# Causal scores of nine blocks in column tiles of 32 keys instead of full 128 x 128 products

## The chip, the cores and the metric

The kernel runs on one core of a Trainium2 chip. The metric is device time in microseconds, the median of several executions. One execution was also recorded by the hardware profiler; its spans and waits are read below.

## The reference

A decayed linear attention feeds two feed-forward layers; the second is a mixture of eight experts of which each token takes one.

```python
# attention, batch 4, heads 8, 768 steps, head size 48
mag = np.sqrt(a_re*a_re + a_im*a_im)
scale = np.minimum(mag, 0.999) / (mag + 1e-06)
ar, ai = a_re*scale, a_im*scale
for t in range(S):
    S_re, S_im = ar*S_re - ai*S_im + kv_t, ar*S_im + ai*S_re   # kv_t = outer(k_t, v_t)
    y[:, :, t] = einsum('bhd,bhde->bhe', q_t, S_re)
x = y as (3072, 384)
# first layer
x = ((x @ w_a) * (x @ w_b)) @ w_out          # inner width 1536
# second layer: 8 experts, inner width 1024, the best one per token
out[token] = gate[token] * (relu(x @ w1[e]) @ w2[e])
```

## The kernel before

Tokens go in 12 blocks of 256 (two chunks of 128), three blocks for each of the four batches. For a block, `pre` works out decays and phases on ScalarE, VectorE and GpSimd, so that the recurrence becomes ordinary products of k and q with 96 rows (real and imaginary part), and SP turns k and q by DMA into `kT` and `qT`, head by head. `attn` then makes, for each chunk:

- `sc`: scores of keys against queries, in two groups (`hg`) of four heads, into one PSUM bank of 128 keys x 4 heads x 128 queries. Keys lie on the partitions. The whole 128 x 128 square is computed.
- `mask`: VectorE multiplies the bank by `causal` (-1 for a query not before the key, else 0), one 128 x 128 triangle repeated for four heads, and writes `sm` in SBUF.
- `kn` and `kept`: TensorE turns k back to keys on partitions, ScalarE copies it out. Not needed for the last chunk of a batch.
- `y`: `sm` times v, plus the state times q, into `y_p`, in four column tiles of 32. v lies in `vpad`, head by head padded to 64 columns.
- `xH`, `xL`: the result is split in two parts, for a product of three fp32r terms.
- `kv`, `sum_`, `fade`: the state of the chunk's end, in three column tiles of 32.

The first layer (`up`, `gate_a`, `gate_b`, `gate_H`, `gate_L`, `down`, 12 slices of the inner width) of block j - 1 runs beside the attention of block j. `sc`, `kn`, `kv`, the counts of the routing and, early, the products that fold the gate's weights into `w_out` (`turned`, `folded`) share one ring of three PSUM banks, `p_sc`. 

The order of the instructions on each engine is worked out when the program is built, by the planner `Plan`. Each operation has an engine, a price, the resources that it reads and writes, and a due time `at`. The planner simulates the engines; among the operations that could start first, it takes the one due first. `TIMES` shifts and stretches the due times of each kind of operation (block 4 stands for all blocks from 4 on). `take` and `give` model the banks of a ring. On the chip the engines keep that order and wait by semaphores. After the planned part, the first layer of the last block, the routing of its tokens and the experts follow, merged by hand.

Of the kernel before, what the change touches and what calls it, by code (L numbers as in the profile page):

```python
# [16 lines left out]
HP = 64  # L17
DM, DFF = 384, 1536
# [49 lines left out]
    'high': (-0, 0.89),  # L68
# [10 lines left out]
    ('pre', 4, 0, 0): (39.6, 1),  # L79
    ('pre', 4, 0, 1): (-35.1, 1),  # L80
    ('pre', 4, 0, 3): (-31.5, 1),
# [379 lines left out]
def fast(tc, q, k, v, a_re, a_im, w_a, w_b, w_out, w_gate, w1, w2, out, dram, x2d):  # L461
# [5 lines left out]
    with ExitStack() as mctx, ExitStack() as ctx:  # L467
# [9 lines left out]
        p_sc = sctx.enter_context(tc.tile_pool(name="p_sc", bufs=3, space=bass.MemoryType.PSUM))  # L477
# [3 lines left out]
        causal = const.tile([128, 128], F32, name="causal")  # L481
        nc.gpsimd.memset(causal, -1.0)
        nc.gpsimd.affine_select(out=causal, in_=causal, pattern=[[1, 128]], compare_op=ALU.is_ge, fill=0.0, base=0, channel_multiplier=-1)
# [42 lines left out]
        def counted():  # L526
            sorting["t"] = p_sc.tile([128, NE], F32, tag="sc", name="so_p")
            nc.tensor.matmul(out=sorting["t"], lhsT=ones16, rhs=acc, start=True, stop=True)
# [72 lines left out]
        def route(j, late):  # L601
# [23 lines left out]
            def count():  # L625
# [10 lines left out]
                t = p_sc.tile([128, 2, NE], F32, tag="sc", name="rk_p")  # L636
# [197 lines left out]
        P = Plan({"sc": 3})  # L834
# [28 lines left out]
        def conv(i, f, src, nm, at):  # L863
# [34 lines left out]
            def turned():  # L898

                K["t"] = p_sc.tile([128, 3, C], F32, tag="sc", name="wt_p")  # L900
                for kk in range(3):
                    nc.tensor.transpose(K["t"][:, kk], A32[nm, f][:, kk * C:(kk + 1) * C], ident)
# [5 lines left out]
            def folded():  # L908
                K["t"] = p_sc.tile([128, NE], F32, tag="sc", name="wg_p")
# [8 lines left out]
            P.add("ACT", on("ACT", 384, True), kept, kind="fold", r=[("wt_p", f)], w=["rx"], at=at + 2, give=t)  # L918
            t = P.add("PE", 0.41, folded, kind="fold", r=["rx"], w=[("wg_p", f)], at=at + 3, take="sc")
            P.add("ACT", 0.17, beside, kind="fold", r=[("wg_p", f)], w=[("A32", nm, f)], at=at + 3, give=t)  # L920
# [39 lines left out]
        def up32(f, cs):  # L960
            n = len(cs) * C
            t = G["ab", 0, f] = p_ab.tile([128, 2, BT], F32, tag="ab", name="ab_p")[:, :, 0:n]
# [4 lines left out]
        def down32(f, cs):  # L967
            for i, c in enumerate(cs):
                if f == 0:
                    G["o", 0, c] = p_o.tile([128, DM + NE], F32, tag=f"o{c}", name=f"o{c}")  # L970
                nc.tensor.matmul(out=G["o", 0, c], lhsT=G["g", 0, f][:, i * C:(i + 1) * C], rhs=A32["o", f], start=f == 0, stop=f == NF - 1)  # L971

        def gate_a32(f, cs):
            n = len(cs) * C
            G["g", 0, f] = mo.tile([128, BT], F32, tag="gL", name="g", bufs=3)[:, 0:n]
            nc.scalar.copy(out=G["g", 0, f], in_=G["ab", 0, f][:, 0])
# [74 lines left out]
        def first_moe(lo, hi):  # L1051
# [10 lines left out]
            for m, (f, cs, at, d) in enumerate(todo):  # L1062
# [3 lines left out]
                P.add("DVE", on("DVE", n), lambda f=f: gate_b(0, f), kind=("gate", 0, cs), r=[a], w=[("gL", m)], at=at, alone=False)  # L1066
# [33 lines left out]
        tpad = [ab.tile([96, H, HP], F32, name=f"T{i}") for i in range(2)]  # L1100
        for t in vpad + tpad:
            nc.gpsimd.memset(t[:, :, D:HP], 0.0)

        SRC = dict(re=a_re, im=a_im, q=q, k=k)

        def load_v(j, c, at):
# [3 lines left out]
            P.add("SP", 0.5, go, kind=("v", min(j, 4)), w=[("v", (2 * j + c) % 3)], at=at, size=196)  # L1110

# [204 lines left out]

        def attn(j, t0, t1):
# [6 lines left out]

            for c in range(2):
# [3 lines left out]
                qk = [(x + "T", c, c2, jj) for x in "qk" for c2 in range(2) for jj in range(3)]  # L1329
                v_, T_, To_ = ("v", (2 * j + c) % 3), ("T", (2 * j + c + 1) % 2), ("T", (2 * j + c) % 2)  # L1330
# [253 lines left out]
```

## Time and profile before

| what | value |
|---|---|
| median of 3 runs | 914.72 us (914.06 to 919.48) |
| profiled execution, its own time | 914.04 us |
| its span, first to last instruction | 912.2 us |
| mean granted TensorE clock | 0.992 |
| TensorE busy | 850.9 us, 93% |
| VectorE, ScalarE, GpSimd busy | 557.2, 477.2, 352.5 us |

Busy time counts how long an engine had something in work; with an engine whose instructions overlap, as TensorE's do, the distance between the starts of two instructions tells more than the listed duration of one. A wait is put down to what released it.

### The profile page before, as it was taken

What the parts mean: (1) busy time and instruction counts of PE and PEld (TensorE: products, weight loads), DVE (VectorE), ACT (ScalarE), POOL (GpSimd) and SP (SyncE); (2) the same over time, 40 slices, a digit from 0 to 9 for tenths busy, and PEclk for the clock granted to TensorE, in tenths of its full rate; (3) what the DMA queues carried; (4) which work ended last, traced back from release to release, by engine and by line L of the source; (5) the groups of instructions that cost most, each with busy time, mean ns of one, the idle gap of its engine ahead of it and who ended that gap; (6) DMA issues with size and microseconds to landing.
All of it is one profiled execution on the core that took longest, in us unless ns stands there. A gap on an engine that the chain in (4) does not pass through costs nothing.

```text
span 912.2 us, 20675 instructions
## 1 busy us (share of the span) xinstructions
PE 850.9 (93%) x8188; PEld 816.7 (90%) x8188; DVE 557.2 (61%) x1217; ACT 477.2 (52%) x887; POOL 352.5 (39%) x338
## 2 busy tenths in 40 slices
PE   0399999999999999999999999999995999999995
PEld 0387899999999999999999999999995999999995
DVE  6999997683838475666757593445731545455540
ACT  6487887574656474655655552224521534344430
POOL 2341441414454545363544444204163343444311
PEclk9999999999999999999999999999997999999998
DMA  9999964433242452627274524123341544454511
GB/s 254 276 279 236 244 142 124 103 90 100 69 96 81 109 170 65 200 60 217 63 208 69 167 59 145 36 88 122 105 153 35 160 133 138 147 161 129 164 51 25
DMA packets 134379, 120.17 MB, mean 132 GB/s; under 512 B 37284, under 2 KB 128820, under 8 KB 134271
## 3 DMA queue, kind: packets, MB, share of 16 engines
q1 hardware_dynamic: 121151, 100.51, 39.3%
q0 software_dynamic: 11392, 17.43, 8.3%
q8 instruction: 67, 1.10, 0.5%
q10 hardware_dynamic: 1728, 0.79, 0.4%
q14 instruction: 41, 0.34, 0.2%
HBM read 82.42 MB, written 10.56 MB: 102 GB/s over the span
## 4 chain that ended last, share of the span: by engine, by line
PE 72%; issue 13%; DMA 5%; POOL 5%; DVE 3%; SPq 1%; ACT 0%; POOLq 0%; DVEq 0%; ACTq 0%
PE ab_p L957 31%; PE o L1000 16%; PE h_p L771 4%; PE sc_p L1335 4%; PE y_p L1374 4%; PE o L803 4%; PE ab_p L965 3%; POOL gt L732 2%; POOL out_dram L814 2%; PE o L971 2%; PE kv_p L1394 2%; DMA out_dram<-ye,ids 1%; PE kn_p L1344 1%; DMA v<-in_v_dram 1%; DMA ids<-idtab 1%
## 5 line engine op out<-in xcount | busy, mean ns | idle before, releaser
L957 PE MATMUL ab_p<-xH,wL 128*128 128x256 f32 x792 | 220.9, 279 | 0.0
L957 PEld LDWEIGHTS ab_p<-xH,wL 128*128 128x128 f32 x792 | 148.8, 188 | 0.0
L991 POOL TENSOR_TENSOR gL<-g,gH 128x256 fp32r<-128x256 f32 x96 | 80.3, 838 | 171.4 <-ACT gH L987 166.9
L980 ACT COPY g<-ab_p 128x256 f32<-128x256 f32 x132 | 48.8, 370 | 133.6 <-PE ab_p L957 124.3
L983 DVE TENSOR_TENSOR g<-g,ab_p 128x256 f32<-128x256 f32 (+1 forms) x148 | 60.7, 410 | 90.3 <-ACT g L980 87.0
L957 PE MATMUL ab_p<-xH,waH 128*128 128x256 f32 x396 | 113.7, 287 | 0.0
L957 PE MATMUL ab_p<-xL,waH 128*128 128x256 f32 x396 | 111.1, 281 | 0.0
L957 PE MATMUL ab_p<-xH,wbH 128*128 128x256 f32 x396 | 110.6, 279 | 0.0
L957 PE MATMUL ab_p<-xL,wbH 128*128 128x256 f32 x396 | 110.4, 279 | 0.0
L1000 PE MATMUL o<-woH,gH 128*128 128x392 f32 x264 | 96.4, 365 | 0.0
L1000 PE MATMUL o<-wL,gH 128*128 128x392 f32 x264 | 90.3, 342 | 0.0
L1000 PE MATMUL o<-woH,gL 128*128 128x392 f32 x264 | 90.2, 342 | 0.0
L771 PE MATMUL h_p<-sH,w1H 128*128 128x256 f32 (+5 forms) x240 | 78.2, 326 | 11.2 <-issue 10.2
L803 PE MATMUL o<-w2H,h 128*128 128x384 f32 (+3 forms) x312 | 86.2, 340 | 0.0
L771 PE MATMUL h_p<-sL,w1H 128*128 128x256 f32 (+5 forms) x240 | 77.4, 323 | 0.0
L771 PE MATMUL h_p<-sH,w1L 128*128 128x256 f32 (+5 forms) x240 | 77.4, 322 | 0.0
L987 ACT ACTIVATE gH<-g 128x256 fp32r<-128x256 f32 x132 | 54.5, 413 | 40.3 <-DVE g L983 36.7
L957 PEld LDWEIGHTS ab_p<-xH,waH 128*128 128x128 f32 x396 | 74.5, 188 | 0.9 <-issue 0.2
L957 PEld LDWEIGHTS ab_p<-xL,waH 128*128 128x128 f32 x396 | 74.6, 188 | 0.4
L957 PEld LDWEIGHTS ab_p<-xL,wbH 128*128 128x128 f32 x396 | 74.5, 188 | 0.0
L957 PEld LDWEIGHTS ab_p<-xH,wbH 128*128 128x128 f32 x396 | 74.4, 188 | 0.0
L814 POOL DMA_INDIRECT out_dram<-ye,ids x29 | 30.2, 1040 | 92.9 <-ACT ye L813 84.2
(210 smaller groups left out, 2162.8 us busy)
## 6 DMA issues: line engine op xcount, KB each, us to landing
raw<-in_moe_w_dram SPq DMA_DIRECT2D x64, 384.0 KB
q<-in_q_dram SPq DMA_DIRECT2D x24, 192.0 KB
v<-in_v_dram SPq DMA_DIRECT2D x24, 192.0 KB
raw<-in_moe_w_a_dram SPq DMA_DIRECT2D x12, 384.0 KB
raw<-in_moe_w_b_dram SPq DMA_DIRECT2D x12, 384.0 KB
raw<-in_moe_w_out_dram SPq DMA_DIRECT2D x12, 384.0 KB
wL<-a POOLq DMA_DIRECT2D x24, 192.0 KB
x2d<-x SPq DMA_DIRECT2D x24, 192.0 KB
```

The lines of the kernel that those rows point to most:

```text
L771: nc.tensor.matmul(out=t, lhsT=lh[:, o:o + 128], rhs=rh[:, kk], start=n == 0, stop=n == 8)
L803: nc.tensor.matmul(out=G["o", c], lhsT=lh, rhs=rh, start=f == 0 and n == 0, stop=f == NH - 1 and n == len(ops) - 1)
L814: d = nc.gpsimd.indirect_dma_start(out, bass.IndirectOffsetOnAxis(ap=ids[0:r, c:c + 1], axis=0), y[0:r], None, bounds_check=NT - 1, oob_is ...
L957: nc.tensor.matmul(out=t[:, i], lhsT=lh[:, kk * 128:(kk + 1) * 128], rhs=rh[:, kk], start=n == 0, stop=n == 8)
L965: nc.tensor.matmul(out=t[:, i], lhsT=A32[nm, f][:, kk * 128:(kk + 1) * 128], rhs=xT["F", 0][:, kk, cs[0]:cs[0] + len(cs)].rearrange("p c t ...
L980: nc.scalar.copy(out=G["g", j, f], in_=G["ab", j, f][:, 0])
L983: nc.vector.tensor_tensor(out=G["g", j, f], in0=G["g", j, f], in1=G["ab", j, f][:, 1], op=ALU.mult)
L987: nc.scalar.activation(out=G["H", j, f], in_=G["g", j, f], func=ACTF.Copy)
L991: eng.tensor_tensor(out=G["L", j, f], in0=G["g", j, f], in1=G["H", j, f].bitcast(F32), op=ALU.subtract)
L1000: nc.tensor.matmul(out=G["o", j, c], lhsT=lh[:, c * C:(c + 1) * C], rhs=rh, start=f == first and n == 0, stop=f == last and n == 2)
L1335: nc.tensor.matmul(out=S["p", hg][:, h], lhsT=pq["k", j][:, hg * 4 + h, c, :], rhs=pq["q", j][:, hg * 4 + h, c, 0:C], start=True, stop=True)
L1374: nc.tensor.matmul(out=t[q4 * 32:q4 * 32 + 32, kk], lhsT=a, rhs=b, start=f0, stop=f1)
```

## The change

From block 3 on (`SWAP`), the scores of a group are made of 16 products instead of four. For a strip of 32 keys that begins at b, and for each of the four heads r, only the queries from b to 127 are multiplied, and the 32 keys go to the partitions that begin at (b + 32 r) mod 128: the four heads of one b lie in four different column tiles. So head r has its keys rotated by 32 r partitions. The part of the bank that is not written holds zeros, which a memset puts there once; for that, two of the three banks are kept for scores (`KEPT`), and `kn`, `kv` and the counts share the one that is left (ring `s1`). The resources "banks" and "kept" order the moment of the change. The mask becomes a tile of four differently rotated triangles in bf16 (`masks`), and it is used as bf16 in the first three blocks too. `y` takes v for heads with r > 0 from `vrot`, which six DMAs per chunk fill with rotated copies (two for each r). The planner's price of a group goes from 0.9 to 0.64, and `TIMES` has other entries for the blocks from 4 on. Some dictionary keys of the first block's layer get the chunk added, which changes no instruction.

```diff
-        p_sc = sctx.enter_context(tc.tile_pool(name="p_sc", bufs=3, space=bass.MemoryType.PSUM))
+        p_sc = sctx.enter_context(tc.tile_pool(name="p_sc", bufs=1, space=bass.MemoryType.PSUM))
+        scores, phase, turns = [], [0], [0, 0]
+
+        def bank(shape, name):
+            if phase[0] == 2:
+                return p_sc.tile(shape, F32, tag="sc", name=name)
+            n = turns[phase[0]]
+            turns[phase[0]] += 1
+            return p_sc.tile(shape, F32, tag=f"s{n % 3}" if phase[0] == 0 else f"s{(turns[0] + n % (3 - KEPT)) % 3}", name=name)
...
-        causal = const.tile([128, 128], F32, name="causal")
-        nc.gpsimd.memset(causal, -1.0)
+        masks = ab.tile([128, 4, C], BF16, name="masks")
+        nc.gpsimd.memset(masks, -1.0)
+        causal = masks[:, 0]
...
+        vrot = [ab.tile([128, 3, 2, HP], F32, name=f"vr{i}") for i in range(3)]
+        for t in vrot:
+            nc.gpsimd.memset(t[:, 0::2, :, 0:HP - D], 0.0)
+            nc.gpsimd.memset(t[:, 1, :, D:HP], 0.0)
+        for r in range(1, 4):
+            n = STRIP * (1 + (r == 2))
+            for a in range(0, C, n):
+                nc.gpsimd.affine_select(out=masks[a:a + n, r], in_=masks[a:a + n, r], pattern=[[1, C]], compare_op=ALU.is_ge, fill=0.0, base=-((a - r * STRIP) % C), channel_multiplier=-1)
+
+        def emptied(i):
+            scores.append(bank([128, 4, C], "scores"))
+            nc.vector.memset(scores[i], 0.0)
...
+            def turned(r, x):
+                def f():
+                    t, n = vrot[(2 * j + c) % 3], r * STRIP
+                    a, b = ((0, n), (n, C))[x]
+                    o, p0 = (HP - D) * (r % 2), (2 * j + c) * C + (a - n) % C
+                    nc.sync.dma_start(out=t[a:b, r - 1, :, o:o + D], in_=v[p0:p0 + b - a, :].rearrange("p (x r d) -> p x r d", r=4, d=D)[:, :, r])
+                return f
+
+            if j >= SWAP:
+                for r in range(1, 4):
+                    for x in range(2):
+                        P.add("SP", 0.5, turned(r, x), kind=("v", min(j, 4)), w=[("vr", (2 * j + c) % 3, r, x)], at=at, early=at, size=12 * (r, 4 - r)[x])
...
+            if j == SWAP:
+                for i in range(KEPT):
+                    P.add("DVE", 0.55, lambda i=i: emptied(i), r=["kept"], w=["banks", ("scores", i)], at=t0 - 10)
+                P.add("SP", 0.0, kept_banks, w=["banks", "kept"], at=t0 - 10)
...
                 def sc(hg, c=c, S=S):
-                    S["p", hg] = p_sc.tile([128, 4, C], F32, tag="sc", name="sc_p")
-                    for h in range(4):
-                        nc.tensor.matmul(out=S["p", hg][:, h], lhsT=pq["k", j][:, hg * 4 + h, c, :], rhs=pq["q", j][:, hg * 4 + h, c, 0:C], start=True, stop=True)
+                    t = S["p", hg] = bank([128, 4, C], "sc_p") if j < SWAP else scores[hg % KEPT]
+                    if j < SWAP:
+                        for h in range(4):
+                            nc.tensor.matmul(out=t[:, h], lhsT=pq["k", j][:, hg * 4 + h, c, :], rhs=pq["q", j][:, hg * 4 + h, c, 0:C], start=True, stop=True)
+                        return
+                    for b in range(0, C, STRIP):
+                        for r in range(4):
+                            a = (b + r * STRIP) % C
+                            nc.tensor.matmul(out=t[a:a + STRIP, r, b:C], lhsT=pq["k", j][:, hg * 4 + r, c, b:b + STRIP], rhs=pq["q", j][:, hg * 4 + r, c, b:C], start=True, stop=True)
...
-                    nc.vector.tensor_tensor(out=S["s", hg], in0=S["p", hg], in1=causal.unsqueeze(1).to_broadcast([128, 4, C]), op=ALU.mult)
+                    nc.vector.tensor_tensor(out=S["s", hg], in0=S["p", hg], in1=masks if j >= SWAP else causal.unsqueeze(1).to_broadcast([128, 4, C]), op=ALU.mult)
...
+                                if h % 4 and j >= SWAP:
+                                    vt = vrot[(2 * j + c) % 3].rearrange("p r x d -> p (r x d)")
+                                    vo = o - h * HP + (h % 2) * (HP - D) + ((h % 4 - 1) * 2 + h // 4) * HP
...
-                    add("PE", 0.9, at_(sc, hg), qk + [("kT", c), ("qT", c)], [("sc_p", j, c, hg)], take="sc")
-                    add("DVE", on("DVE", 512), at_(mask, hg), [("sc_p", j, c, hg)], [("sm", hg)], give=True, alone=False)
+                    if j < SWAP:
...
+                    else:
+                        p_ = ("scores", hg % KEPT)
+                        add("PE", 0.64, at_(sc, hg), qk + [("kT", c), ("qT", c)], [p_])
+                        add("DVE", on("DVE", 512), at_(mask, hg), [p_], [("sm", hg)], alone=False)
...
-    ('attn', 4, 'PE'): (4.8735, 1),
-    ('attn', 4, 'DVE'): (-34.6, 1),
-    ('attn', 4, 'ACT'): (-22.9, 1),
-    ('up', 4): (-11.3, 1),
-    ('gate', 4): (-41.3, 1),
-    ('down', 4): (-9.1, 1),
+    ('attn', 4, 'PE'): (-1.6265, 1),
+    ('attn', 4, 'DVE'): (-132.3, 1),
+    ('attn', 4, 'ACT'): (-138, 1),
+    ('up', 4): (-5.2, 1),
+    ('gate', 4): (-134.8, 1),
+    ('down', 4): (-5.1, 1),
```

## Rows read from the trace of the kernel before

**Rows 1.** The page, span in 40 equal slices, busy tenths; PEclk is the granted clock.

```profile
PE   0399999999999999999999999999995999999995
PEclk9999999999999999999999999999997999999998
```

**Rows 2.** Table by stretches of 25 us: busy time of each engine, clock, DMA share.

```profile
400.00:425.00 25.00, 25.00 (x285) 24.22 (x284) 10.22 (x25) 10.93 (x23) 12.65 (x12) 1.00 0.45 125
...
675.00:700.00 25.00, 14.81 (x94) 14.60 (x93) 3.86 (x8) 3.69 (x9) 13.99 (x14) 0.80 0.35 107
```

**Rows 3.** Waits of TensorE's weight loads, 150 to 640 us: total, times, longest.

```profile
PEld o L1000 <- issue: 3.2, 16, 0.2
...
PEld o L1000 <- ACT kn L1349: 0.2, 1, 0.2
```

**Rows 4.** Timeline of TensorE around a score group: start, duration, line.

```profile
306.73 0.28 PE L957 MATMUL ab_p<-xH,wL 128*128 128x256 f32 x1
306.85 1.05 PE L1335 MATMUL sc_p<-qT,kT 96*128 96x128 f32 x8
307.66 0.43 PE L1000 MATMUL o<-woH,gH 128*128 128x392 f32 x1
307.93 0.34 PE L1000 MATMUL o<-wL,gH 128*128 128x392 f32 x1
308.10 0.34 PE L1000 MATMUL o<-woH,gL 128*128 128x392 f32 x1
```

**Rows 5.** Timeline of TensorE around a y product with state.

```profile
211.75 0.34 PE L1000 MATMUL o<-woH,gL 128*128 128x392 f32 x1
212.02 0.43 PE L1374 MATMUL y_p<-sm,v 128*32 128x128 f32 x8
...
212.49 0.40 PE L1374 MATMUL y_p<-sm,v 128*32 128x128 f32 x8
...
213.59 0.40 PE L1374 MATMUL y_p<-qT,T 96*32 96x128 f32 x8
213.92 0.44 PE L1000 MATMUL o<-woH,gH 128*128 128x392 f32 x1
214.20 0.34 PE L1000 MATMUL o<-wL,gH 128*128 128x392 f32 x1
```

**Rows 6.** Timeline of TensorE around a kv product that stands alone.

```profile
214.92 0.34 PE L1000 MATMUL o<-woH,gL 128*128 128x392 f32 x1
215.19 0.88 PE L1394 MATMUL kv_p<-v,kn 128*32 128x48 f32 x48
216.01 0.39 PE L957 MATMUL ab_p<-xH,waH 128*128 128x256 f32 x1
216.23 0.28 PE L957 MATMUL ab_p<-xL,waH 128*128 128x256 f32 x1
```

**Rows 7.** Timeline of TensorE around the folding product, 8 columns in four tiles.

```profile
93.06 0.38 PE L912 MATMUL wg_p<-wg,wt 128*32 128x8 f32 x24
93.36 2.86 PE L965 MATMUL ab_p<-x,a 128*128 128x256 f32 x12
```

**Rows 8.** Lines by themselves: minimum, median, maximum in ns; first and last start.

```profile
L1339 DVE TENSOR_TENSOR sm<-sc_p,causal x48: 657/692/694, 41.4 to 602.2; 128x512 f32<-128x512 f32 x48
...
L1109 SPq DMA_DIRECT2D v<-in_v_dram x24: 553/594/1513, 5.6 to 540.0; - x24
...
L1349 ACT COPY kn<-kn_p x40: 457/479/500, 45.7 to 583.4; 128x384 f32<-128x384 f32 x40
```

**Rows 9.** Timeline of GpSimd at the start: a select, the first square.

```profile
1.47 0.28 POOL L483 TENSOR_SCALAR_AFFINE_SELECT causal<-causal 128x128 f32<-128x128 f32 x1
...
4.97 0.83 POOL L1201 TENSOR_TENSOR Bt<-im 128x384 f32<-128x384 f32 x1 [1.65 <-DMA im<-in_a_im_dram]
```

**Rows 10.** Timeline of VectorE at the start, the sum behind that square.

```profile
5.83 0.56 DVE L1177 TENSOR_TENSOR Bt<-A,Bt 128x384 f32<-128x384 f32 x1 [4.29 <-POOL Bt L1201]
```

More of the change, by code (lines that the diff above doesn't have):

```diff
@@ L526, in counted @@
         def counted():
-            sorting["t"] = p_sc.tile([128, NE], F32, tag="sc", name="so_p")
+            sorting["t"] = bank([128, NE], "so_p")
             nc.tensor.matmul(out=sorting["t"], lhsT=ones16, rhs=acc, start=True, stop=True)
@@ L635, in count @@
                     base = eoff
-                t = p_sc.tile([128, 2, NE], F32, tag="sc", name="rk_p")
+                t = bank([128, 2, NE], "rk_p")
                 for c in range(2):
@@ L898, in turned @@
             def turned():
-                K["t"] = p_sc.tile([128, 3, C], F32, tag="sc", name="wt_p")
+                K["t"] = bank([128, 3, C], "wt_p")
                 for kk in range(3):
@@ L908, in folded @@
             def folded():
-                K["t"] = p_sc.tile([128, NE], F32, tag="sc", name="wg_p")
+                K["t"] = bank([128, NE], "wg_p")
                 for kk in range(3):
@@ L917, in conv @@
             t = P.add("PE", 0.45, turned, kind="fold", r=[slot], w=[("wt_p", f)], at=at + 2, take="sc")
[L918 removed]
+            P.add("ACT", on("ACT", 384, True), kept, kind="fold", r=[("wt_p", f), "banks"], w=["rx"], at=at + 2, give=t)
             t = P.add("PE", 0.41, folded, kind="fold", r=["rx"], w=[("wg_p", f)], at=at + 3, take="sc")
[L920 removed]
+            P.add("ACT", 0.17, beside, kind="fold", r=[("wg_p", f), "banks"], w=[("A32", nm, f)], at=at + 3, give=t)
         def parted(i, f, nm, at):
@@ L970, in down32, with gate_b32 @@
                     G["o", 0, c] = p_o.tile([128, DM + NE], F32, tag=f"o{c}", name=f"o{c}")
-                nc.tensor.matmul(out=G["o", 0, c], lhsT=G["g", 0, f][:, i * C:(i + 1) * C], rhs=A32["o", f], start=f == 0, stop=f == NF - 1)
+                nc.tensor.matmul(out=G["o", 0, c], lhsT=G["g", 0, f, cs][:, i * C:(i + 1) * C], rhs=A32["o", f], start=f == 0, stop=f == NF - 1)
         def gate_a32(f, cs):
             n = len(cs) * C
-            G["g", 0, f] = mo.tile([128, BT], F32, tag="gL", name="g", bufs=3)[:, 0:n]
-            nc.scalar.copy(out=G["g", 0, f], in_=G["ab", 0, f][:, 0])
+            G["g", 0, f, cs] = mo.tile([128, BT], F32, tag="gL", name="g", bufs=3)[:, 0:n]
+            nc.scalar.copy(out=G["g", 0, f, cs], in_=G["ab", 0, f, cs][:, 0])
+        def gate_b32(f, cs):
+            nc.vector.tensor_tensor(out=G["g", 0, f, cs], in0=G["g", 0, f, cs], in1=G["ab", 0, f, cs][:, 1], op=ALU.mult)
         def gate_a(j, f):
@@ L1390, in kv @@
                 def kv(c=c, S=S):
-                    t = S["kv"] = p_sc.tile([96, H, D], F32, tag="sc", name="kv_p")
+                    t = S["kv"] = bank([96, H, D], "kv_p")
                     for h in range(H):
@@ L1426, in attn @@
                 if not last:
-                    add("PE", 0.82, kv, [("kn", 0), ("kn", 1), v_], [("kv_p", j, c)], take="sc")
-                    add("DVE", on("DVE", 384), sum_, [("kv_p", j, c), T_] + qk, [To_], give=True, alone=False)
+                    add("PE", 0.82, kv, [("kn", 0), ("kn", 1), v_, "kept"], [("kv_p", j, c)], take=ring(j))
+                    add("DVE", on("DVE", 384), sum_, [("kv_p", j, c), T_, "banks"] + qk, [To_], give=True, alone=False)
                     add("DVE", 0.01 if first else on("DVE", 384), fade, [To_] + qk, [To_])
@@ L1495, in fast @@
             P.add("DVE", 0.9, pick, r=[("lgt", j % 2, 0), ("lgt", j % 2, 1)], w=["oh"], at=at)
-            t = P.add("PE", 0.2, count, r=["oh", "acc"], w=["rk_p"], at=at + 2, take="sc")
-            P.add("DVE", 1.1, place, r=["rk_p", "oh"], w=["acc", "posu"], at=at + 2, give=t)
+            t = P.add("PE", 0.2, count, r=["oh", "acc", "kept"], w=["rk_p"], at=at + 2, take=ring(j))
+            P.add("DVE", 1.1, place, r=["rk_p", "oh", "banks"], w=["acc", "posu"], at=at + 2, give=t)
             for c in range(2):
@@ L1510, in fast @@
             P.run()
+        phase[0] = 2
+        sctx.close()
+        p_sc = sctx.enter_context(tc.tile_pool(name="p_sc1", bufs=3, space=bass.MemoryType.PSUM))
+        P2[0] = p_sc
         cvctx.close()
```

41 lines of the change are left out of this document (28 added, 13 removed).

## The prediction

> **What bounds the kernel now.** I read the page first: the busy tenths put TensorE at 9 in nearly every slice after the second, at the full granted clock [rows 1]. The table by stretches says the same more sharply: from 400 to 425 us TensorE is busy for all 25.00 us, VectorE for 10.22, ScalarE for 10.93; the one stretch after the start with a hole is 675 to 700, where 14.81 us are busy [rows 2]. Then the waits of TensorE's weight loads between 150 and 640 us: the largest group is 3.2 us over 16 times, none longer than 0.2, and those have no releaser; the only wait for a copy out of the shared score banks is 0.2 us [rows 3]. So from block 3 on, TensorE's own instruction stream sets the time, in the order in which it stands. A microsecond less in that stream is a microsecond less at the end; a microsecond less on any other engine is nothing. What counts is therefore not how long a score matmul is listed as busy, but how far the start of the next piece moves. I read that from the timeline, start to start.
>
> **A score group as it is.** One group is four fp32 matmuls of 128 queries, 8 records. At 306.85 it begins one step of 0.12 after the up product before it (no gap); 0.81 later, at 307.66, the down product begins, whose first step is 0.27 where its steady step is 0.17 [rows 4]. So a group takes 0.81 + 0.09 = 0.90 us of the stream. Blocks 3 to 11 hold 9 blocks x 2 chunks x 2 groups = 36 groups, 32.4 us.
>
> **The same group in column tiles.** The change makes 16 matmuls (32 records), four each with 128, 96, 64 and 32 queries. No such product is in the trace, but three kinds in four or three column tiles of 32 are. The y product moves 128 queries: its sets of 8 records start at 212.49 and, five sets later, at 213.59, so 0.22 a set and 27.5 ns a record [rows 5], about a quarter of the score group's 101 ns: column tiles of different heads do run beside each other. The kv product moves 48 columns in three column tiles, 48 records in 0.82 us, 17 ns each with its end counted in [rows 6]; the small folding product moves 8 columns, 24 records in 0.30 us, 12.5 ns [rows 7]. I scale the y rate by the queries and let nothing go below 12.5 ns: 8 x 27.5 + 8 x 20.6 + 8 x 13.8 + 8 x 12.5 ns = 0.60 us.
>
> That would save 0.30 us a group. But going from full-width products into column tiles and back is not free, and this is the step on which the forecast turns. The y product starts at 212.02, where the step before it would have ended at 211.75 + 0.18 = 211.93; it holds the stream until 213.92, and the next product's first step is 0.28 instead of 0.18 [rows 5]. Together 0.09 + 1.90 + 0.10 = 2.09 us for 64 records, of which 64 x 27.5 ns = 1.76 is streaming: 0.33 us for one excursion. The kv product shows it again: 0.09 before, 0.10 in the first step after (216.01 to 216.23 against 0.12) [rows 4, 6]. The score group ends on narrow strips, whose three staggered neighbours drain in about 3 x 12.5 ns rather than 3 x 27.5, so I take 0.05 off: 0.28. Rows alone give 0.60 + 0.28 = 0.88 us. The planner's own new weight for it is 0.64, by the convention that puts y at 1.9, which is its start to start; with the 0.09 and 0.10 around it that is 0.83. I take 0.85, between them. **The term:** 36 x (0.90 - 0.85) = 1.8 us less. Bounds: no excursion price at all gives 36 x (0.90 - 0.64) = 9.4 less; streaming at 0.60 and the full 0.33, 36 x 0.03 = 1.1 more.
>
> Whether excursions can be shared depends on the order. The planner takes among ready operations the one due first. In the new due times the first group of a chunk is due at lo + 1.4 and the second at lo + 3.9, and an up product (lo + 2.3) and a down product (lo + 2.9) are due in between; y and kv also lie between an up and a down. So nearly every group is alone, as now (in blocks 5 to 11 one down product stands between the two). Were all groups in pairs, a pair would take 2 x 0.60 + 0.28 = 1.48 against 1.78 for two neighbours now, 18 x 0.30 = 5.4 us less.
>
> **The other parts.** The mask product is still 512 elements per partition out of PSUM, 692 ns [rows 8]; its second operand is now bf16 and not repeated. No row shows that form, so I bound it by a gain or a loss of a tenth of the 692 ns; VectorE, at 10.22 us of 25 in the quiet stretches [rows 2], hides it: nothing. Weights of the rotated heads come from another tile, same shape: nothing.
>
> The rotated copies of v are six small DMAs a chunk, 108 in all, on SP's queue behind the load of v. The load of v takes 594 ns of SP to issue [rows 8]; the new ones have 64 to 192 of its 1024 runs of 192 bytes, so they lie between a sixteenth of that and all of it, 0.04 to 0.6 us each; I take 0.4, 43 us of SP spread over 450. They are due a block ahead and wait only for the y of three chunks earlier. Behind them on SP stand the transposes of k and q, and the loads of the next block; SP moves nothing that is late today on TensorE's list [rows 3]. I cost them at nothing; without the cover 0 to 3 us.
>
> At the start GpSimd gets ten more selects (0.28 us each, some 0.25 apart, as the one for the triangular mask [rows 9]), six more memsets and a longer one: about 3.5 us before the first square of im, which today has 1.65 us of slack, waiting for its DMA [rows 9]. So the first half starts about 1.9 us later. VectorE waits 4.29 us for that square's sum and has smaller holes until the weight conversion fills it [rows 10], so I charge 0.4 us of 0 to 1.9.
>
> The banks: three shared banks become, from block 3 on, two for scores and one for the rest. Two memsets of 512 elements and a drain of earlier users stand at the change, covered by up products: 0.2 us, 0 to 2. After it kn, kv and the counts pass one bank from hand to hand: 15 chunks with state x 3 uses, 9 counts, 1 last = 55 uses. A use is held by the copy of kn, 479 ns on ScalarE [rows 8], or its like on VectorE. Between the uses stand up and down products of 1.1 to 2.1 us in the due order, and ScalarE is idle more than half the time [rows 2]. I charge 0.2 us in all; 0.1 us at every use is 5.5.
>
> **The sum.** The profiled execution took 914.04 us (span 912.2, 1.84 around it), 0.68 below the median of 914.72. 914.04 - 1.8 + 0.4 + 0.2 + 0.2 = 913.0 us. The hole of about 10 us near 684 comes from gathers that follow the last block, so I let it move along unchanged.
>
> **Rivals.** (a) The excursion is cheaper than y's or is shared, because groups stand together or next to y and kv: between pairs, 914.04 - 5.4 + 0.8 = 909.4, and no price at all, 914.04 - 9.4 + 0.8 = 905.4. For it: the planner's 0.64; against it: y and kv pay every time. (b) Narrow strips go out no faster than wide ones: 32 x 27.5 ns = 0.88, with 0.28 it is 1.16, 36 x 0.26 = 9.4 more, 914.04 + 9.4 + 0.8 = 924.2, slower. It decides as soon as the 24 records of 32 to 96 queries take more than 16.7 ns on average, where 0.22 + 24 x 0.0167 + 0.28 = 0.90; my sum has 15.6, so the sign of the term hangs on little. Against it stand the 12.5 ns of the folding product and the 14 ns of kv without its excursion, (1.01 - 0.33) / 48 [rows 6, 7]. The Trainium skill has a rule of this kind (TensorE: Matmul & The Clock Gate, section "Wait — 56ns, not 53.3ns?"): starts never come closer than about 25 ns, however few columns move. By it, as an estimate, the group would be 0.22 + 0.60 + 0.28 = 1.10 and the kernel about 922; the rows of kv and folding are below 25 and speak against it for column tiles. (c) The single bank makes TensorE wait: 55 uses at 0.1 to 0.2 us are 5.5 to 11 more, 917 to 923. Against it: one wait of 0.2 today, but with three banks [rows 3]. (d) The four strips don't overlap, each alone at the score group's rate: 2560 columns instead of 1024 in 0.81 us are 2.03, with 0.28 it is 2.31, 36 x 1.41 = 51 more, 965; y speaks against it.
>
> **How the numbers follow.** Forecast, 911.5 to 915: 0.52. (a) 0.22, of it 0.08 below 905.6. (b) 0.05, (c) 0.18, (d) 0.03. Range: 905 to 918; it leaves out (d), (b), the upper half of (c) and a rest of (a), some 0.2. One per cent (905.6 and 923.9) is about what a measurement of this kernel can tell from no change. Faster by more than it 0.08, within it 0.85, slower 0.07.
>
> **What would show it.** In the timeline after: 32 records a score group, about 0.64 us start to start, and a first step of 0.22 to 0.28 in the product behind it. A first step of 0.12 or 0.18 there, or groups side by side, would be (a). Steps of 27 ns in the narrow strips would be (b); weight loads or matmuls waiting for the copy of kn or the sum of kv would be (c). GpSimd's first square later than 4.97 us would show the start. The forecast fails most easily on the excursion price, which is read from products that end on wider tiles.

## The result and the profile after

The changed kernel took **922.38 us**, median of 11 runs (918.74 to 927.39), the kernel before 915.12 beside it (11 runs, 912.98 to 919.48): ratio 1.0082, 95% interval 1.0061 to 1.0103. I had forecast 913.0 in a range of 905 to 918. It is slower by 0.8%, in the band of "within 1%", but outside the range. The profiled execution took 926.28 us, one of the longer of its eleven, with a span of 924.5; so the two profiled executions lie 12.3 us apart in their spans, where the medians lie 7.3 apart.

First the score groups, for the whole forecast hung on them. TensorE around a group that stands alone, timeline of after (start, duration, line):

```profile
198.23 0.34 PE L1018 MATMUL o<-woH,gL 128*128 128x392 f32 x1
198.50 0.76 PE L1395 MATMUL scores<-qT,kT 96*32 96x128 f32 x32
199.19 0.44 PE L1018 MATMUL o<-woH,gH 128*128 128x392 f32 x1
199.47 0.34 PE L1018 MATMUL o<-wL,gH 128*128 128x392 f32 x1
```

It begins 0.09 behind the 198.41 at which the step before it would have ended, holds the stream for 0.69, and the next first step is 0.28 instead of 0.18: 0.09 + 0.69 + 0.10 = 0.88 us, the sum by rows to the hundredth, against 0.90 [rows 4]. Of the groups that stand alone there are over 20, at 0.88 to 0.90. Six pairs stand back to back, one of them here:

```profile
287.50 0.28 PE L972 MATMUL ab_p<-xH,wL 128*128 128x256 f32 x1
287.71 1.32 PE L1395 MATMUL scores<-qT,kT 96*32 96x128 f32 x64
288.96 0.45 PE L1018 MATMUL o<-woH,gH 128*128 128x392 f32 x1
289.25 0.34 PE L1018 MATMUL o<-wL,gH 128*128 128x392 f32 x1
```

0.09 + 1.25 + 0.11 = 1.45 us, where I had 1.48. The two together give the parts: a pair holds one excursion (entering the column tiles and leaving them) and two groups, so the excursion is 2 x 0.88 - 1.45 = 0.31 us and a group streams in 0.57; I had 0.28 and 0.60. So the scores did what the rows said. The time went elsewhere, and the first up product of a block says where (timeline of TensorE, us):

| | before | after | difference |
|---|---|---|---|
| block 1, first half | 117.66 | 122.42 | +4.8 |
| block 1, second half | 136.62 | 142.89 | +6.3 |
| block 2, first half | 165.69 | 177.15 | +11.5 |
| block 11, first half | 606.27 | 617.40 | +11.1 |
| span | 912.2 | 924.5 | +12.3 |

Nearly all of the loss, 11.5 of 12.3 us, lies **ahead of the blocks that the change is about** (the attention of block 3 runs beside the first layer of block 2). From block 2 to block 11 the kernel takes 440.25 us where it took 440.58; behind that it loses 1.2 more. The page shows the places at once: in the third slice (46 to 69 us) and in the seventh (139 to 162) TensorE is at 8 tenths, in the seventh its granted clock too, where before it was 9 in both [rows 1].

```profile
PE   0389998999999999999999999999995999999995
PEclk9999998999999999999999999999997999999998
```

The table by stretches of after, against [rows 2], and behind it one stretch of before. Each row has the stretch and its length; busy us and instructions of TensorE's products, TensorE's weight loads, VectorE, ScalarE and GpSimd; the granted clock, the DMA share and GB/s:

```profile
150.00:175.00 25.00, 22.64 (x294) 22.12 (x295) 17.52 (x36) 14.74 (x24) 3.58 (x2) 0.86 0.29 79
400.00:425.00 25.00, 25.00 (x332) 23.80 (x331) 13.14 (x30) 10.98 (x21) 15.83 (x12) 1.00 0.37 86
```

```profile
150.00:175.00 25.00, 25.00 (x298) 24.30 (x287) 20.03 (x40) 15.84 (x27) 6.89 (x5) 1.00 0.21 55
```

At 400 us nothing is wrong. From 150 to 175 TensorE is idle for 2.36 us and its granted clock is 0.86, where before it was busy throughout at 1.00. The waits of TensorE's matmuls from 20 to 640 us (total, times, longest) name what it waited for. The longest, 34.8 us for weights at the start, was 33.9 in before and is left out:

```profile
...
PE ab_p L972 <- DVE g L1001: 3.4, 3, 1.6
PE sc_p L1390 <- DMA qT<-q: 3.0, 1, 3.0
...
PE ab_p L980 <- ACT x L1444: 2.0, 1, 2.0
```

The longest of the waits for a gate, 1.6 us, stands at 131.90, between the two halves of block 1, where the table goes from 4.8 to 6.3. The 3.0 us are block 2's first scores, old and full-width, waiting for a turn of q. SP's queue ahead of them:

```profile
101.36 10.01 SPq L1150 DMA_DIRECT2D vr<-in_v_dram  x8
...
142.58 3.49 SPq L1332 DMA_DIRECT2D qT<-A  x2
146.17 1.21 SPq L1332 DMA_DIRECT2D qT<-q  x2
147.55 0.47 SPq L1172 DMA_DIRECT2D k<-in_k_dram  x1
148.06 0.55 SPq L1332 DMA_DIRECT2D qT<-q  x1
```

The load of block 3's k (384 KB) stands between the second and the last turn of block 2's q; TensorE starts those scores at 152.36. In before that load stood behind the last turn, at 141.94, and TensorE waited 0.43 us:

```profile
140.16 1.26 SPq L1286 DMA_DIRECT2D qT<-q  x2
141.94 0.40 SPq L1126 DMA_DIRECT2D k<-in_k_dram  x1
```

```profile
143.52 1.13 PE L1335 MATMUL sc_p<-qT,kT 96*128 96x128 f32 x8 [0.43 <-issue]
```

And eight of the new loads of rotated copies take up 10 us of SP's queue in the stretch of the weight loads, and v, q and k of block 2 stand behind them.

The smaller terms, as lines of after: the mask product (a mean of 687 ns, against a median of 692 in [rows 8]), the loads of the copies, and GpSimd's start (against [rows 9]).

```profile
L1399 DVE TENSOR_TENSOR sm<-scores,masks 128x512 f32<-128x512 f32 x36 | 24.4, 687 | 9.7 <-PE scores L1395 8.8 <-PE kn_p L1404 0.8
```

```profile
L1150 SPq DMA_DIRECT2D vr<-in_v_dram x108: 555/594/1568, 72.8 to 541.8; - x108
```

```profile
4.06 3.39 POOL L1128 TENSOR_SCALAR_AFFINE_SELECT masks<-masks 32x128 bf16<-32x128 bf16 x10
7.54 0.82 POOL L1247 TENSOR_TENSOR Bt<-im 128x384 f32<-128x384 f32 x1
```

### The profile page after: what moved, and what is told of

It is laid out like the page before. It is cut to its first block, busy times and chain, and to the rows that moved or that the text cites. A ratio compares the mean times of both kernels' runs of the same rounds, so it can differ in the third digit from the quotient of the medians.

```text
span 924.5 us, 22585 instructions
## 1 busy us (share of the span) xinstructions
PE 855.5 (93%) x9052; PEld 810.0 (88%) x9052; DVE 563.8 (61%) x1219; ACT 478.9 (52%) x887; POOL 356.4 (39%) x354
## 4 chain that ended last, share of the span: by engine, by line
PE 66%; issue 15%; POOL 6%; DVE 5%; DMA 4%; ACT 1%; SPq 1%; ACTq 0%; POOLq 0%; DVEq 0%
PE ab_p L972 29%; PE o L1018 15%; PE y_p L1439 4%; PE ab_p L980 3%; PE h_p L786 3%; PE scores L1395 3%; PE o L818 2%; POOL gt L747 2%; POOL out_dram L829 2%; PE kv_p L1459 2%; PE o L986 1%; DMA out_dram<-ye,ids 1%; PE kn_p L1404 1%; PE sc_p L1390 1%; DMA ids<-idtab 1%
## 5 line engine op out<-in xcount | busy, mean ns | idle before, releaser
L972 PE MATMUL ab_p<-xH,waH 128*128 128x256 f32 x396 | 116.5, 294 | 3.4 <-DVE g L1001 3.4
L1001 DVE TENSOR_TENSOR g<-g,ab_p 128x256 f32<-128x256 f32 x132 | 54.8, 416 | 102.7 <-ACT g L998 101.5
```

Of the source, the lines that this page charges most:

```text
L972: nc.tensor.matmul(out=t[:, i], lhsT=lh[:, kk * 128:(kk + 1) * 128], rhs=rh[:, kk], start=n == 0, stop=n == 8)
L1001: nc.vector.tensor_tensor(out=G["g", j, f], in0=G["g", j, f], in1=G["ab", j, f][:, 1], op=ALU.mult)
```

## The experiments

They ran on other chips, one for each batch: e1 to e6; e7 to e10; e11 to e13 with the changed kernel; e14 to e16; e17 to e19. The kernel before was measured beside each and takes 898.8 to 899.5 us there (its hole near 684 is not there: in e6 TensorE is busy for all 25.00 us from 675 to 700). A ratio compares with before on the same chip. It comes with its 95% interval and is not the quotient of the two medians; the two can differ by over 1 us. A difference between two batches crosses chips, and before alone varies by 0.7 us between them. "Block time" below is the time from block 2's to block 11's first up product in the one profiled run of a kernel, 439.46 us for the full-score order of before (e6).

**The start, and the loads in the stretch of the weight loads.** First theory, A: the ten selects and the memsets delay the first chunk. Rival, B: the rotated loads on SP delay the next loads. In e1 to e3 the same work is emitted later on its engine; e6 adds the work of the start to the kernel before.

```
# e1: masks[:, 1:4], vrot memsets and the ten selects
+    if (j, c, hg) == (2, 0, 0): prepared()
# e2: the six loads of a chunk, on SP, at its first score group
-    P.add("SP", 0.5, turned(r, x), ...)
+    P.add("SP", 0.5, lambda: held[(j, c)].append(turned(r, x)), ...)
+    if hg == 0: for f in held.pop((j, c), ()): f()
# e6: the kernel before, with the selects and masks added and not read
```

> The changed kernel with GpSimd's ten selects, the memsets of vrot and three quarters of the memset of masks emitted at block 2's first score group instead of ahead of the first square; the order of every engine is otherwise that of the changed kernel. Theory A (the loss is at the head: the first square starts 2.6 us late, and TensorE's clock falls in the gap near 49 us): the first square is back at 4.97 us, the first score group near 39.4, the clock stays whole near 49 us, and the kernel takes 915 to 918 us, some 4 to 5 less than the changed kernel's 922.4; a wait for the transposes of block 2's q near 150 us may stay. Theory B (the loss comes from the single bank and the new order of blocks 3 to 11): 920 to 923, unchanged.

> The changed kernel with the six loads of a chunk's rotated v moved on SP's queue to the point where that chunk's first score group is emitted; nothing else is moved, the start is as in the changed kernel. Theory A: SP is free between 72 and 119 us again, so the loads of block 3's k and q go out some 15 us earlier and the wait for block 2's turned q near 150 us is gone in every run; the loss at the head stays: 918 to 919.5, with little spread. Theory B (single bank, new order from block 3): 920 to 923.

> Both moves of the two kernels before at once: prepared late and rotated loads late. Theory A: both losses at the head and near 150 us are gone, what is left is the stretch from block 3 on, which by the accounting of starts gains about 2.2 us (24 groups alone at 0.89 instead of 0.90, six pairs at 1.46 instead of 1.78) and loses about as much in new waits: 912.5 to 915. Theory B: 920 or more.

> The kernel before with only the ten selects on a tile of four masks and its memset added on GpSimd ahead of the first square; the results of these are not used and scores are made as before. Theory A: 917 to 919.5, 3 to 4.5 more than before, though the added work is only 3.9 us on an engine that is busy 39% of the time. Theory B, and the step of the prediction that charged 0.4 us for this: 914.5 to 915.5.

Measured: e1 907.31 us, ratio 1.0083 (1.0057 to 1.0109); e2 905.65, 1.0057 (1.0039 to 1.0074); e3 905.71, 1.0056 (1.0040 to 1.0072); e6 899.57, 0.9998 (0.9984 to 1.0012). The changed kernel itself was measured later, beside e11 to e13:

> The changed kernel itself on this chip. Theory: what the single moves gave adds up: 6.2 us for the kernel with both moves of the start (e3_both against before), 2.4 more for the rotated loads in the stretch of the weight loads (e1_prep_late less e3_both by their ratios), 0 for the selects (e2_vr_late against e3_both, and e6): 899.5 + 8.6 = 908, ratio 1.0095, within 2 us. A rival: the selects do cost here together with the rest, 910 to 912.

It took 908.0, ratio 1.0100 (1.0083 to 1.0117). In its profiled run it comes to block 1 2.8 us later than e6 and to block 2 6.5 us later, and its block time is 442.36, 2.9 more than e6's: here a part of the loss lies in the blocks, as it didn't in the run above.

**Theory A is not borne out as a term of its own**: e2 and e3 differ only in the place of the selects and memsets (first square at 7.53 and at 5.18 us), and by 0.06 us in the median. That doesn't show that a late square is free. In the traces e2 comes to block 1 3.6 us later than e3 and to block 2 1.1 us earlier, for its wait in front of block 2's first scores, the subject of the next part, is 2.1 us where e3's is 3.8. Every run with the late square has that wait. And e6 doesn't test theory A: there GpSimd makes the selects behind the first square, which comes in time.

```profile
4.92 0.82 POOL L1207 TENSOR_TENSOR Bt<-im 128x384 f32<-128x384 f32 x1 [1.13 <-DMA im<-in_a_im_dram]
5.71 4.32 POOL L1108 TENSOR_SCALAR_AFFINE_SELECT masks<-masks 32x128 bf16<-32x128 bf16 x10
```

B holds for a part: with the loads moved out of the weight loads the time falls by 908.0 - 905.65 = 2.35 us (e2, another chip than the changed kernel's) and by 907.31 - 905.71 = 1.6 us (e1 to e3, one chip, but five runs of e1 and ratios whose intervals overlap). One place of it shows in the traces: in block 1 TensorE waits 0.9 us for a gate in the changed kernel and 0.8 in e1, and not at all in e2 and e3. The larger part of the loss was still there in e3.

**The load of k and the last turn.** In e3 TensorE waits 3.8 us ahead of block 2's first scores, with the same order on SP as above:

```profile
PE sc_p L1398 <- DMA k<-in_k_dram: 3.8, 1, 3.8
```

Theory C: that one load costs it. The move, and its opposite in the kernel before:

```
# e7 = e3 and, in loads: block 3's k is put off ...
+    if (nm, j) == ("k", 3) and sent[0] < 12: late.append(f); return
# ... and issued in turn(jj) behind the twelfth turn of block 2
+    while sent[0] == 12 and late: late.pop()()
# e8 = before: the last turn of block 2's q put off until that load
+    if (src, c2, jj, j) == ("q", 1, 2, 2) and not kahead: late.append(f); return
```

> e3_both with one move on SP's queue: the load of k for block 3 (384 KB) stands behind the twelfth turn of block 2 and no longer between the second and the last turn of the rotated q. Theory C (what is left of the loss after e3 is this load ahead of the last turn: TensorE waits 3.8 us for it at 143.8 and then runs two score groups and the products beside them at the lower clock): the wait falls below 1.5 us, the granted clock of 145 to 155 us is whole, the loss of 5.6 us between 137 and 172 us goes, ratio to before 0.999 to 1.002. Rival (the loss belongs to the score change or to the banks and only shows at this place): the ratio stays at 1.0056.

> The kernel before with the opposite move alone: the last turn of block 2's rotated q stands behind the load of k for block 3. Nothing of the score change is in it. Theory C: TensorE waits 2.5 to 4 us more ahead of block 2's first scores, the clock falls behind it, and the kernel is 3 to 5.5 us slower, ratio 1.003 to 1.006. Rival (the place is covered, as the same order in blocks 5 to 10 of before is): ratio 0.999 to 1.001.

e7 took 903.12, ratio 1.0027 (1.0011 to 1.0043): 2.6 less than e3, not the 5 that I expected. e8 took 904.05 against 899.46, ratio 1.0050 (1.0033 to 1.0066), as expected. Stretches of 5 us, e3:

```profile
145.00:150.00 5.00, 2.42 (x10) 2.45 (x11) 2.14 (x5) 4.93 (x8) 4.60 (x15) 0.72 0.55 157
150.00:155.00 5.00, 5.00 (x24) 4.96 (x24) 2.86 (x5) 0.66 (x1) 3.29 (x5) 0.59 0.25 79
```

The same of e7:

```profile
145.00:150.00 5.00, 4.27 (x31) 3.97 (x31) 2.05 (x5) 4.92 (x9) 2.91 (x10) 1.00 0.77 214
150.00:155.00 5.00, 5.00 (x132) 4.78 (x132) 4.12 (x7) 3.87 (x6) 4.45 (x10) 1.00 0.41 114
```

And e8, its wait, its stretches and SP's queue:

```profile
PE sc_p L1344 <- DMA k<-in_k_dram: 3.5, 1, 3.5
```

```profile
145.00:150.00 5.00, 2.48 (x14) 2.50 (x15) 1.57 (x3) 3.02 (x4) 0.00 (x0) 0.90 0.55 169
150.00:155.00 5.00, 5.00 (x64) 4.84 (x66) 4.15 (x7) 1.35 (x3) 0.00 (x0) 0.76 0.32 88
```

```profile
143.28 0.40 SPq L1128 DMA_DIRECT2D k<-in_k_dram  x1
143.72 0.55 SPq L1295 DMA_DIRECT2D qT<-q  x1
```

The delay has two parts. TensorE begins the scores 2.1 us after the end of the last turn's issue in before (141.42 to 143.52), 3.25 in e8 (144.27 to 147.52) and 3.8 in e3 (143.79 to 147.58). And the issue of that turn is held back: in e8 SP is done with the turn before it at 142.11, and the load of k goes out only at 143.28; in e3 that gap is 0.2 us.

In the trace the place is settled. From block 1's second half to block 2, e3 lost 5.65 us against e6, e7 loses 0.13, and e8, with not one score product changed, loses 4.26. TensorE's hole is followed by some microseconds at the lower clock: 0.59 of the full clock is a mean of the two levels (1.2 and 2.4 GHz), and a full-width score group there takes 2.05 us instead of 1.13. In the median e7 gained only half of that. Its profiled run comes to block 1 2.7 us later than e3's, of which more below; whether that is so in its other runs was not measured.

**The score products by themselves.** e10 undoes them alone, e13 undoes only the triangle, e9 brings the groups together.

```
# e9 = e7, both groups of a chunk at the first one's place
+    if j >= SWAP and hg == 0: sc1(0); sc1(1)
# e10 = e7, full products, causal mask, all of y from the plain v
-    if j < SWAP:
+    if True:
# e13 = e9, every strip over all 128 queries
-    out=t[a:a + STRIP, r, b:C] ... rhs=...[:, ..., b:C]
+    out=t[a:a + STRIP, r, 0:C] ... rhs=...[:, ..., 0:C]
```

> e7_k_last with both score groups of a chunk back to back at the first one's place, in blocks 3 to 11: 18 pairs where there are 6. The price of entering and leaving the column tiles is then paid once a chunk. Theory (a pair is 1.46 us and two groups alone are 1.78): 12 x 0.32 = 3.8 us less than e7_k_last, ratio about 0.996. Rival (the gates behind the pair come late, TensorE waits for them, and gives it back): within 1 us of e7_k_last.

> e7_k_last with the score products of before (four of 128 x 128 a group) in blocks 3 to 11, the triangular mask, and all heads' y from the plain copy of v: the output is the reference's, and the order, the banks and the loads of the rotated copies stay. Theory (a group in column tiles costs the stream 0.88 to 0.90, as the full one does, and only 6 pairs save 0.32 each): 0 to 2 us slower than e7_k_last. Rival by the start to start of the score products alone: 5.3 us slower.

> e9_k_last_pairs with every strip of 32 keys over all 128 queries: the part above the diagonal is made too and the mask sets it to zero, so the output is the reference's. 32 records a group as before, 2048 columns where there were 1280. Theory (a record of a strip costs its columns, 27.5 ns for 128 queries, down to 12.5): a group is 0.88 of streaming in place of 0.60, 36 x 0.28 = 10 us slower than e9_k_last_pairs, ratio about 1.011. Rival (narrow strips go out no faster than wide ones): the same time as e9_k_last_pairs.

| | median us | ratio (95%) | block time us |
|---|---|---|---|
| e7 | 903.12 | 1.0027 (1.0011 to 1.0043) | 439.97 |
| e10, full products | 904.59 | 1.0048 (1.0031 to 1.0065) | 443.17 |
| e9, 18 pairs | 899.82 | 0.9993 (0.9975 to 1.0012) | 436.60 |
| e13, 18 pairs, no triangle | 910.41 | 1.0136 (1.0113 to 1.0159) | 447.74 |

The change's own products are worth 1.5 us by the medians and 3.2 by the block times (one chip; the intervals of the two ratios overlap). Twelve more pairs give 3.3 us by both (3.8 expected), and the triangle is worth 10.6 or 11.1 (10 expected). A wide pair in e13:

```profile
279.47 0.28 PE L972 MATMUL ab_p<-xH,wL 128*128 128x256 f32 x1
279.68 1.95 PE L1407 MATMUL scores<-qT,kT 96*32 96x128 f32 x64
281.56 0.45 PE L1018 MATMUL o<-woH,gH 128*128 128x392 f32 x1
281.85 0.35 PE L1018 MATMUL o<-wL,gH 128*128 128x392 f32 x1
```

0.09 + 1.88 + 0.11 = 2.08 us against 1.45. Without the 0.31 of the excursion that is 1.77 / 64 = 28 ns a record against 1.14 / 64 = 18 ns, and the 24 narrower records of a group take (0.57 - 0.22) / 24 = 14.6 ns on average, below the 16.7 at which I had the term change its sign. Rival (b) is refuted. The Trainium skill (TensorE: Matmul & The Clock Gate, "Wait — 56ns, not 53.3ns?") has starts never closer than about 25 ns. For records in column tiles the trace doesn't agree: 18 ns.

**The wait for a gate in block 4.** What did e10, with the products of before, lose in its blocks, 3.7 us against e6? 2.7 are two waits of up products for a gate product on VectorE, one of 1.4 in block 4, near 265 us (1.8 in e9). There the decay of the state stretches beside a GpSimd product, with the gate behind it. VectorE and GpSimd in e9:

```profile
262.11 0.55 DVE L1490 TENSOR_TENSOR T<-T,kv_p 96x384 f32<-96x384 f32 x1 [0.97 <-PE kv_p L1482]
262.70 2.08 DVE L1496 TENSOR_TENSOR T<-T,qT 96x384 f32<-96x384 f32 x1
264.70 0.41 DVE L1001 TENSOR_TENSOR g<-g,ab_p 128x256 f32<-128x256 f32 x1
```

```profile
262.55 1.80 POOL L1329 TENSOR_TENSOR Bt<-k,X 128x768 f32<-128x768 f32 x1
```

The decay is 0.55 us elsewhere. Theory D: put it behind the gate, and the wait of 1.8 us goes.

```
# e11 = e9, e12 = e7: in fade, for (j, c) == (4, 1)
+    faded.append(lambda: fade(True)); return
# in gate_b, behind the product
+    while faded: faded.pop()()
# e14 = e12, e15 = e11: behind the third gate product
```

> e9_k_last_pairs with one move on VectorE's queue: in the second chunk of block 4 the decay of the state (T times its column of q, 0.55 us elsewhere, 2.08 us here, beside a product of the next block's k on GpSimd of 1.80) stands behind the next gate product instead of ahead of it. Theory D (the gate product waits behind the stretched decay, and TensorE's up product waits 1.8 us for it): the wait of TensorE for the gate near 265 us goes, 1.5 to 2.3 us less than e9_k_last_pairs, ratio to before about 0.997. Rival (the copy and the low half that follow come no earlier): no difference.

> e7_k_last with the same move of the decay, without the pairs: the changed kernel as it is, apart from the places of the start's preparation, the rotated loads, the k load and this decay. Theory: 1.5 to 2 us less than e7_k_last (903.1), 901 to 901.5, ratio 1.000 to 1.002: what is left of the score change itself, about 3.5 us less by the trace, against what the new order and banks cost. Rival: as e7_k_last, 1.0027.

> e12_fade with the decay of block 4's second chunk behind the third gate product instead of the first, where GpSimd has finished its product of k. In e12_fade the decay took 4.09 us beside three GpSimd products in a row, and TensorE waited 0.9 for a gate and 0.9 for the turn of k. Theory D (the decay must not stand beside GpSimd's products with a gate behind it): the decay takes 0.55 to 1, no wait for the gate near 270 us, 1.5 to 2.5 us less than e7_k_last and e12_fade: 900.5 to 901.5, ratio 1.001 to 1.002. Rival: as those two, 1.003.

> e11_pairs_fade with the decay behind the third gate product. In e11_pairs_fade the decay still takes 2.14 us, but TensorE waits only 0.4 there. Theory D: 0 to 0.6 us less than e11_pairs_fade, ratio 0.996 to 0.997; the first measurement of e11_pairs_fade is repeated with it. Rival: what e11_pairs_fade gained was an accident of its runs, and this one stands at 0.999.

| | median us | ratio (95%) | block time us |
|---|---|---|---|
| e11 | 896.26 | 0.9970 (0.9955 to 0.9985) | 435.00 |
| e12 | 902.67 | 1.0034 (1.0020 to 1.0047) | 440.65 |
| e14 | 904.20 | 1.0047 (1.0029 to 1.0065) | 440.59 |
| e15 | 898.68 | 0.9994 (0.9979 to 1.0009) | 436.79 |

D holds in one order of four: in e11 the wait for a gate falls from 1.8 to 0.5 us, the block time by 1.6 and the median by 3.6 (1.5 and 2.6 when both were run again, below), so that about half of the gain isn't placed. In e12 the decay meets three GpSimd products in a row:

```profile
267.20 4.09 DVE L1497 TENSOR_TENSOR T<-T,qT 96x384 f32<-96x384 f32 x1
271.21 0.41 DVE L1003 TENSOR_TENSOR g<-g,ab_p 128x256 f32<-128x256 f32 x1
```

```profile
266.53 1.84 POOL L1333 TENSOR_TENSOR Bt<-k,X 128x768 f32<-128x768 f32 x1
268.32 0.74 POOL L1013 TENSOR_TENSOR gL<-g,gH 128x256 fp32r<-128x256 f32 x1
269.02 1.84 POOL L1333 TENSOR_TENSOR k<-k,X 128x768 f32<-128x768 f32 x1
```

In e14 it is down to 0.78, the wait near 265 us is gone, and the block time is as it was: TensorE now waits 1.0 us for a turn of block 5's k and 1.2 in all for gates, 0.8 of it at 274.87. So that wait was not the only one that was due there; taking it away uncovers the next.

**The loads and the due times in blocks 3 to 11.**

```
# e16 = e10 without the 108 loads, which it does not read
-    for f in held.pop((j, c), ()): f()
# e17 = before with the whole changed table of due times, blocks 4 to 11
#       (it moves loads, turns and pre too)
```

> e10_k_last_full without the 108 loads of the rotated copies of v, which it does not read: scores in full products, order and banks of the changed kernel, output the reference's. If the loads themselves cost time in blocks 3 to 11 (their issue on SP ahead of the turns), it is 1 to 3 us faster than e10_k_last_full; by my reading (they are covered there, and what costs is the order and the place of GpSimd's products) it is the same within 0.7 us, ratio about 1.0045.

> The kernel before with nothing but the changed table of due times (blocks 4 to 11); full score products, three shared banks, no rotated copies. e10_k_last_full, with the same products and the changed order and banks, lost 3.8 us between block 2's and block 11's end, up to 2.7 of it waits for a gate. If the due times cause that, this kernel is 2.5 to 4 us slower than before, ratio 1.003 to 1.0045, with a wait of an up product for a gate near 262 us; if the single bank and the kept ones cause it, it is within 1 us of before.

e16 took 903.68, ratio 1.0043 (1.0028 to 1.0057), block time 443.18 against 443.17: there the loads cost nothing. e17 took 901.64, ratio 1.0037 (1.0025 to 1.0050): **the due times alone cost 2.6 us** by the medians (six runs of e17). The mechanism that I expected is not there: e17 has no wait of an up product for a gate in its blocks (its one such wait, 0.8 us, lies ahead of 172 us, and e6 has it too). Its profiled run places 0.7 us in the blocks and 0.5 behind them; the rest isn't placed. So of the 3.7 us that e10 loses in its blocks the due times explain 0.7. The two waits for a gate come with something else of the change. The single bank, with the order that is planned around it, is a rival that no run tests.

**A version that beats both.** e11 and its neighbour e9, once more:

> e11_pairs_fade once more, the same kernel. It stood 3.2 us below before and 3.6 below e9_k_last_pairs, while its trace is only 1.6 us shorter than e9's between block 2 and block 11, and e15_pairs_fade_third gave that back. If its gain is real, ratio 0.996 to 0.998 again; if an accident of the runs, 0.999, beside e19_pairs_again.

> e9_k_last_pairs once more, the same kernel, beside e18_pairs_fade_again: ratio 0.999 to 1.000, and 1 to 2 us above e18 if the move of the decay helps.

e18 took 897.21, ratio 0.9978 (0.9965 to 0.9992), e19 899.80, 1.0009 (0.9993 to 1.0024). So the changed scores in pairs, with k's load behind the last turn, the loads of the copies at their chunk and the decay behind one gate, are faster than before by 0.2 to 0.3% and than the changed kernel (908.0) by 1.2 to 1.3%.

## Why the prediction was wrong

**The step that failed** stands under "The other parts": the rotated copies on SP, "SP moves nothing that is late today on TensorE's list [rows 3]. I cost them at nothing; without the cover 0 to 3 us." It failed twice. [rows 3] begins at 150 us, and the two places at which SP is late lie ahead of it: the weight loads, at 70 to 117 us, and block 2's turns, at 130 to 143. In before TensorE already had a hole of 0.43 us in front of these scores, at 143.52, so there was no cover. And a planned queue doesn't take 108 loads as an addition at the end: it sorts them in by due time, and in the changed kernel the order of the others is another. The last turn came to stand behind a load of 384 KB. Not shown is what of the change moved it there; with the due times alone (e17) the load still goes out behind the last turn, at 142.58. The price: 1.6 to 2.35 us for the copies in the weight loads; for the order, 4.6 by e8, 2.6 by e7 against e3, 5.5 by the trace at the place. Rival (c), which ended on the slow side, was a wait too, but for the shared bank; no wait for a copy out of it is in the trace.

**Left out of the sum**: the new due times. I used them to see where the score groups come, and charged nothing for what they do to the rest, though the diff moves gates and mask products by some 100 us. e17 prices them at 2.6 us, of which its trace places 1.2.

**The score term**: -1.8 forecast; 1.5 (medians) and 3.2 (block times) measured by e7 against e10; by the groups, 6 pairs x 0.35 and 24 alone x 0.01 are 2.3. That it is near is luck. I took 0.05 for each of 36 lone groups, by going down from my own 0.88 to 0.85; a lone group gives 0.01, and the gain comes from the six pairs, which I had put under rival (a) and not into the sum. The lone group itself, the point on which I said that the forecast turns, held: 0.88 by rows, 0.88 measured, with a part of 0.03 too little in the excursion and as much too much in the streaming.

**Right as costed**: the mask (687 ns against 692); the copies in the blocks (594 ns each on SP, above the 0.4 that I took, and still hidden, by e16). For the banks no wait for a copy is in the trace, but what the single bank does to the order is not priced. The start: the first square came 2.57 us later (7.54 against 4.97 [rows 9]), not 1.9, for the selects took 0.34 us each; of that TensorE's first product shows 0.40 (26.68 against 26.28), the 0.4 that I charged. What it is worth at the end no run shows by itself.

**The account**, on the later chips: 1.6 to 2.35 for the copies, 2.6 to 4.6 for the order on SP, 2.6 for the due times, 2.3 less for the scores: 4.5 to 7.2 of the 8.5 us measured. Its terms come from separate kernels and need not add. **What stays open**: 3 us of what e10 loses in its blocks, and the first 60 us. Two profiled runs of one kernel (e9 and e19) reach block 1's products 3.9 us apart and agree in block time (436.60 and 436.58). The traces with the changed code come there 1.2 to 5.8 us later than e6, those of e8 and e17, relatives of before, 1.4 and 0.7; a wait that differs is the one for the copy of the first x (0.3 us in e6, 2.8 in e7), but e10 comes 1.8 later without it. One or two us of the loss may lie there; by what, the runs don't tell. On the first chip, the profiled run lost its 4.8 us in steps: 1.0 up to the first scores (40.35 against 39.36), 2.6 up to the first up product, behind a wait of 2.0 for that copy (1.2 in before), and 4.2 at 53.15 (48.99 in before), behind products at a lower granted clock (0.50 from 50 to 52 us).

## What to carry to other kernels

Where a planner orders the queues, an added operation is priced by the order that comes out, not by its own duration: compare the queue's order before and after around every place where the busiest engine is fed just in time, and look at those places from the first microsecond on. An array mode that costs an entry and an exit of 0.31 us pays when its products stand together: the same products were worth 1.5 to 3 us with most groups alone and 3.3 more in pairs. A wait that is taken away is worth what the next one leaves of it: e14 removed its own and gained nothing.

## What the runs showed of the hardware

- A VectorE product with both operands in SBUF (96 x 384, 0.55 us alone) ended only when GpSimd's product of two SBUF operands beside it had ended: 2.08 us beside one (e9), 4.09 beside three in a row (e12: 1.84, 0.74 and 1.84 us), two of which started after it. In e11 it came in behind the first of such a row (2.14 us), and the GpSimd product behind it took 1.06 us instead of 0.74. The Trainium skill (SBUF — State Buffer, section "SBUF: two separate sides") has the shared port as an exclusive lock for whoever comes first. The trace agrees that one blocks the other, and shows besides that the loser can stay blocked through the products that follow.
- A hole of 3.5 to 3.8 us in TensorE's stream, which ended near 147.5, was followed by a granted clock of 0.59 to 0.76 from 150 to 155 us (e3, e8); behind a hole of 0.7 it was 1.00 (e7).
- Column tiles of 32 with 128, 96, 64 and 32 queries stream at 18 ns a record on average, of 128 queries each at 28.
- TensorE began the scores that wait for a turn of q 2.1 us after the end of its issue when a load of 384 KB stood behind it on SP's queue (before), and 3.25 to 3.8 us after when that load stood ahead of it (e8, e3).
